# Attention with a window and sinks, then an MLP mixer, on one core: q and k of two more head pairs turned by TensorE, with new orders of work

## The chip, the core and the metric

The kernel runs on one core of a Trainium2 chip. Its engines are TensorE (PE in the profile; PEld is its weight load), VectorE (DVE), ScalarE (ACT), GpSimd (POOL) and SyncE (SP), beside sixteen DMA engines that all queues share. The metric is the device time of one execution in microseconds, the median of several runs. A profiled execution has its own time and, inside it, a span from its first to its last instruction.

## The reference, cut to what matters

```python
# q, k, v: (4, 8, 768, 64) float32, n_sink = 4, window = 128
scores = scale * np.matmul(q, k.transpose(0, 1, 3, 2))
is_sink = pos[None, :] < int(n_sink)
rel = pos[:, None] - pos[None, :]
in_window = (rel >= 0) & (rel < int(window))
scores = np.where(is_sink | in_window, scores, -1000000000.0)
a = softmax(scores);  attn = np.matmul(a, v)         # softmax written out in the reference
x = attn.transpose(0, 2, 1, 3).reshape(4, 768, 512)
h = np.maximum(x.transpose(0, 2, 1) @ w_tok1, 0.0) @ w_tok2   # (512, 768)->(512, 256)->(512, 768)
u = x + h.transpose(0, 2, 1)
out = u + np.maximum(u @ w_ch1, 0.0) @ w_ch2         # 512 -> 1536 -> 512
```

## The kernel before, in words

Work on the attention goes by **pairs** of heads: pair p is batch p // 4 and two of its eight heads, so there are 16 pairs and each batch has four. For a pair, q and k (two heads of 768 rows and 64 columns) are needed turned, with the 2 x 64 columns on the partitions: tiles qT and kT of 128 x 768. Only a band of the scores is computed, three groups g per pair (`scores`), with a further burst for the four sink keys of two pairs at once (`score_sinks`). ACT takes the exponential, DVE masks, and the values follow (`sink_values`, `values`, or `pv` for the first four pairs); DVE divides by the sums and writes x.

After a batch's four pairs come the mixer's steps: `mix_h` and `mix_u` over tokens (u is x plus the result), u is turned to uT, then `v1` (12 x 2 units of four 128x384 products, ReLU on ACT or DVE) and the output product `whole` (24 units of three 128x512 products, added to u by DVE and stored by SP).

**How tiles are turned.** Pairs 0 to 3 arrive by SP as float32 and are cast. From pair 4 on POOL issues loads that cast to bf16 on the way (`load_cast`, L131, two DMAs of 96 KB for q and two for k). Pairs 4 to 7 are turned by TensorE: `transposed` writes 24 small transposes to PSUM (L549), and each of the four quarters of a pair is copied out by ACT (L153) or DVE (L155), the sink columns too (kTs). Pairs 8 to 15 are turned by one DMA each for q and k, which SP issues (L476); the sink columns are then copied out of kT by POOL or DVE (kTs<-kT), so that copy waits in its engine's queue for the DMA to land. The constant `BY_DMA` is the first pair that is turned so; it also sets how the rows of a pair lie over the partitions (`rows_of`: six neighbouring rows in one partition below it, rows 128 apart from it on). u of batches 2 and 3 is turned by DMAs too (L866), that of batches 0 and 1 by TensorE.

**What sets the order.** TensorE's units run in the order of the string `ORDERED`: a letter names a stream and a number the unit in it.

- t, m, s, o: turns, masks, scores and values of pairs 0 to 3; g, h: tokens of batch 0
- a: scores of pairs 4 to 15, three for each, so a12 to a14 are pair 8 and a18 to a20 pair 10
- b: seven for each two pairs: sink scores, then for both pairs sink values and two of values; b0 to b6 are pairs 4 and 5, b14 to b20 pairs 8 and 9
- e: turns by TensorE from pair 4 on: e0 and e1 are q and k of pair 4, e2 pair 5, e3 pair 6, e4 pair 7
- f: u of batch 1 turned; k: tokens of batches 1 to 3, eight each
- c: v1, 24 for each batch; x: output products, 24 for each batch

The loads on POOL go in the order of the string `LOADED`: t is a weight of the tokens, c and d are quarters of w_ch1 and w_ch2, q, k and v with a number are a pair's tiles. q and k have six buffers each (`NQ`), so the load of pair p waits until pair p - 6 has been turned; v has six as well and waits for the values of pair p - 6. POOL has at most eight of its DMAs under way: it waits for the landing of the eighth before. kT has three buffers.

Everything that is not TensorE's (evictions, masks, loads, DMA turns, stores) is put on its queue by a planner, `Plan`: it walks the TensorE order with a cost for each piece and always issues next what can begin first. Its only use is to fix the order in which each engine's instructions are written; each engine then runs its own in that order. A DMA turn costs `TURN` = 1300 ns there, times `CROWDED` while loads are queued.

Of the kernel before, what the change touches and what calls it, by code (L numbers as in the profile page):

```python
# [16 lines left out]
def kernel(  # L17
# [23 lines left out]
    NHP = H // 2  # L41
# [3 lines left out]


    ORDERED = (
# [10 lines left out]
    )  # L58
    ORDER = (1, 2, 7, 6, 4, 5, 3)
    NQ = 6  # L60
    LOADED = (
        "v1 t0 v3 v2 t1 q4 k4 c3 q5 c0 k5 c2 v4 d1 k7 k6 v5 c1 q6 q7 d0 v6 q8 d2 k9 k8 v7 d3 q9 k11 v8 q13 k10 v9 "
        "k15 v12 q10 k14 q11 k12 q12 v10 v11 v13 q14 v14 k13 q15 v15"
    )
    BY_SEVEN = ()
    BY_DMA = 2 * NHP
    MASKED_BY_PE = [(p, g) for p in range(NHP) for g in range(NT // 2) if (p, g) != (NHP - 1, 0)]

    singles = ctx.enter_context(tc.tile_pool(name="singles", bufs=1))
# [17 lines left out]
    def bank(tag, *shape, dtype=FP32, slot=None):  # L87

        n = given[tag].pop(0) if slot is None else slot
        if tag == "sc":  # L90
            return sc[n]
        size = 1
        for x in shape:
            size *= x
        flat = sc[n // 2][:, n % 2].rearrange("p b c d -> p (b c d)")
        flat = (flat if dtype == FP32 else flat.bitcast(dtype))[:, 0:size]
        names = "abc"[:len(shape)]
        return flat.rearrange(
            f"p ({' '.join(names)}) -> p {' '.join(names)}", **{x: v for x, v in zip(names, shape)},
        )  # L100

    in_order = tc.keep_in_program_order
    pairs = [(b, hp) for b in range(B) for hp in range(NHP)]


    def rows_of(pidx, n):

        b, hp = pairs[pidx]
        rows = (q, k)[n][b, 2 * hp:2 * hp + 2]
        if pidx >= BY_DMA:  # L110
            return rows.rearrange("h (j p) d -> p h j d", p=P)
# [33 lines left out]
    def mm(*args, **kwargs):  # L145
        in_order(nc.tensor.matmul(*args, skip_group_check=True, **kwargs))  # L146
# [4 lines left out]
    def copy(e, out, in_):  # L151
        if e == "ACT":
            in_order(nc.scalar.activation(out, in_, AF.Copy))  # L153
        else:
            in_order({"DVE": nc.vector, "POOL": nc.gpsimd}[e].tensor_copy(out=out, in_=in_))  # L155
# [98 lines left out]
    FIRST = 1800.0  # L254
    LANES = 8
    TURN, STORE = 1300.0, 700.0
    CROWDED = 2.4

# [21 lines left out]
    class Plan:  # L280
# [90 lines left out]
        def run(self, units):  # L371
            units = list(units)
            while units or self.pending:
                o = self.other()
                t = self.start_pe(units[0][1]) if units else None
                if o is not None and (t is None or o[0] <= t):
                    op = self.pending.pop(o[1])
                    op.fn(o[2])
                    self.free[o[2]] = o[0] + op.cost[o[2]]
                    op.done = self.free[o[2]] + op.lag  # L380
                    if op.traffic:
                        crowded = self.queue > self.free["SP"] + 1000.0
                        self.sent = max(self.sent, self.free["SP"]) + op.traffic * (CROWDED if crowded else 1.0)
                        self.queue = max(self.queue, self.free["SP"]) + op.traffic
                        op.done = self.sent + 600.0
                    if op.loads:
                        self.queue = max(self.queue, self.free[o[2]] + FIRST) + op.lag
                        op.done = self.queue + 500.0
                        self.landings += [op.done] * op.loads
                    continue  # L390
                assert t is not None, "no unit can begin"
                self.commit_pe(units.pop(0)[1], t)
# [55 lines left out]
    def prepare(p):  # L448
# [22 lines left out]
        tiles["kT", p] = kT  # L471
        if p >= BY_DMA:
            def turn(e, n):
                if not n:
                    tiles["qT", p] = att_pool.tile([P, S], BF16, name="qT2")
                in_order(nc.sync.dma_start_transpose(  # L476
                    out=(kT if n else tiles["qT", p]).rearrange("c (t p) -> c t p", t=NT),
                    in_=bfs[p, n].rearrange("p t h d -> p (t h d)"),
                ))
# [305 lines left out]
    def group(b, g):  # L785
        return g * DM // 2, DM // 2
# [50 lines left out]
    def mix_u(b, g, s0, n, by_pe=False):  # L837
        c0, cn = group(b, g)

        def run():  # L840
            ps_u = tiles["ps_u", b, g, s0] = bank("mx", n, cn)
            for st in range(n):
                if by_pe:
                    mm(ps_u[:, st], ident, x_sb[b][:, s0 + st, c0:c0 + cn], start=True, stop=False)
                for tt in range(NTOK):
                    mm(
                        ps_u[:, st], w_tok2[:, tt, ts(s0 + st, P)], tiles["mix", b][0][:, tt, c0:c0 + cn],
                        start=(tt == 0 and not by_pe), stop=(tt == NTOK - 1),
                    )

        def add(e):
            if by_pe:
                return copy(e, u_part(b, g, s0, n), tiles["ps_u", b, g, s0])
            in_order(nc.vector.tensor_tensor(  # L854
                out=u_part(b, g, s0, n), in0=tiles["ps_u", b, g, s0], in1=x_sb[b][:, s0:s0 + n, c0:c0 + cn], op=ALU.add,
            ))

        op = Op({"DVE": 150.0 + 1.05 * n * cn}, add)
        op.urgent = (1 + g) * (b == 0)
        if by_pe:  # L860
            op.cost["ACT"] = 190.0 + 0.78 * n * cn
        done["u", b, g, s0] = op
        then = [op]
        if pairs[BY_DMA][0] <= b:
            def turn(e):
                in_order(nc.sync.dma_start_transpose(  # L866
                    out=tiles["mix", b][2].rearrange("c (g t p) -> c g t p", g=2, p=P)[:, g, 2 * s0:2 * (s0 + n)],
                    in_=u_part(b, g, s0, n).rearrange("p t c -> p (t c)"),
                ))

            then.append(Op({"SP": 1230.0}, turn, [op], traffic=TURN))
            for half in range(s0 // QH, (s0 + n - 1) // QH + 1):
                done.setdefault(("uT", b, half), []).append(then[-1])
        return unit(n * (NTOK + by_pe) * cn * 0.432, run, done["h", b, g] + [done["tok2"]], {"mx": [[op]]}, then)
# [71 lines left out]
    def attention_and_tokens():  # L946

        scored, out, turns, turned, tokens = [], [], [], [], []
        first, end = NHP, len(pairs)
        for p in range(first, end):  # L950
            prepare(p)
            plan.pending.append(sink_rows(p))
        turns += [turn(first, n) for n in range(2)]
        turns += [burst(transposed(p)) for p in range(first + 1, BY_DMA)]
        for p in range(first, end):
            scored += [burst(scores(p, g)) for g in range(NT // 2)]
            if p % 2:
                out.append(burst(score_sinks(p)))
                for n in (p - 1, p):
                    out += [burst(sink_values(n)), *(values(n, i) for i in range(2))]  # L960
        for b in range(1, B):
            for g in range(2):
                tokens.append(mix_h(b, g, 0, NTOK))
                tokens += [mix_u(b, g, st, 2) for st in range(0, NT, 2)]
                if pairs[BY_DMA][0] > b:
                    turned.append(burst(turned_u(b, g)))
        return scored, out, turns, turned, tokens

# [372 lines left out]
```

## Time and profile before

| | |
|---|---|
| median of 3 runs | 207.49 us (206.03 to 208.84) |
| time of the profiled execution | 208.19 us |
| its span | 206.4 us, 4881 instructions |
| PE busy | 197.1 us (95%), 2021 matmuls |
| DVE, ACT, POOL busy | 106.1, 101.9, 72.0 us |
| mean granted TensorE clock | 0.987 |
| DMA | 26.28 MB in 92550 packets |
| loads issued by POOL, issue to landing | 7.7 to 9.1 us (medians of the q, k, v and w_ch groups) |
| DMA turns of q and k, issue to landing | 7.5 and 8.2 us (medians) |
| DMA turns of u, issue to landing | 2.4 us (median) |

How to read it: PE is nearly always busy, so the end is set by what PE has to do and by the few places where it waits. The other engines matter where PE waits for them. The time of an execution is its span and some 1.8 us around it.

### The profile page before, as it was taken

The page shows a single profiled execution, that of the slowest core. Times are in us where ns is not written, and L with a number is a line of the kernel's source. Part 1 is how long each engine was busy: PE and PEld are TensorE (multiplying, and loading weights), DVE is VectorE, ACT ScalarE, POOL GpSimd, SP SyncE. Part 2 cuts the span into 40 slices and gives each one's busy share as a digit, 9 for nine tenths or more (in the row PEclk, how much of TensorE's full clock was granted, in tenths as well). Part 3 has the DMA queues.
Part 4 walks back from the last instruction along what each step waited for, and adds up shares of the span by engine and source line. Part 5 has one row for each costly group of instructions (what it writes and reads, how often), then busy time and mean ns, then how long its engine had stood idle before and what let it go on. Part 6 is the DMA issues. An engine that isn't in the chain of part 4 may idle for free.

```text
span 206.4 us, 4881 instructions
## 1 busy us (share of the span) xinstructions
PE 197.1 (95%) x2021; PEld 115.4 (56%) x2021; DVE 106.1 (51%) x240; ACT 101.9 (49%) x176; POOL 72.0 (35%) x106
## 2 busy tenths in 40 slices
PE   6999998999995999999999999999999999999992
PEld 2345894566562565566656474566665455654451
DVE  4586877657873637266466776537612423001221
ACT  4598667877860351378754433486551003763000
POOL 6479868997815993676000000000000000000000
PEclk9999999999999699999999999999999999999998
DMA  6999999999999999999995764300122421100223
GB/s 209 253 274 179 175 186 181 175 173 175 125 144 127 222 135 181 180 167 174 138 87 114 156 154 95 137 0 3 37 44 68 110 102 51 54 0 0 102 102 105
DMA packets 92550, 26.28 MB, mean 127 GB/s; under 512 B 82544, under 2 KB 89584, under 8 KB 92528
## 3 DMA queue, kind: packets, MB, share of 16 engines
q0 software_dynamic: 67232, 11.80, 74.9%
q1 hardware_dynamic: 25296, 14.17, 30.4%
q8 instruction: 16, 0.26, 0.5%
q14 instruction: 6, 0.05, 0.1%
HBM read 26.75 MB, written 6.29 MB: 160 GB/s over the span
## 4 chain that ended last, share of the span: by engine, by line
PE 78%; DMA 18%; POOL 1%; SPq 0%; issue 0%; DVE 0%
PE ps L146 76%; DMA q_f<-in_q_dram 6%; DMA kT<-k_bf 5%; DMA w_tok<-in_moe_w_tok_dram 4%; DMA k_bf<-in_k_dram 4%; PE ps L549 1%; PE ps L519 0%; SPq L118 0%; POOL k_bf L131 0%; POOL q_bf L155 0%; POOL w_ch L164 0%; PE ps L149 0%; DVE o_sb L1175 0%
## 5 line engine op out<-in xcount | busy, mean ns | idle before, releaser
L146 PE MATMUL ps<-w_ch,v1T 128*128 128x512 bf16 (+2 forms) x312 | 69.4, 369 | 0.0
L146 PE MATMUL ps<-uT,w_ch 128*128 128x384 bf16 x384 | 68.6, 326 | 0.0
L159 ACT ACTIVATE v1T<-ps 128x384 bf16<-128x384 f32 x78 | 37.8, 491 | 41.2 <-PE ps L146 38.0
L620 ACT ACTIVATE pT<-ps 128x1024 bf16<-128x1024 f32 (+1 forms) x48 | 44.1, 956 | 22.3 <-PE ps L146 22.2
L146 PEld LDWEIGHTS <-w_ch 128*128 128x128 bf16 x384 | 35.8, 98 | 23.4 <-issue 0.7
L146 PEld LDWEIGHTS <-v1T 128*128 128x128 bf16 x312 | 29.2, 99 | 28.4 <-issue 1.9
L1140 DVE TENSOR_TENSOR o_sb<-ps,u_sb 128x512 f32<-128x512 f32 x23 | 15.8, 688 | 38.1 <-PE ps L146 24.0
L131 POOL DMA_DIRECT2D q_bf<-in_q_dram x24 | 19.9, 836 | 5.8 <-DMA v_aug<-in_v_dram 3.2
L146 PEld LDWEIGHTS <-w_tok 128*128 128x128 bf16 x192 | 18.2, 98 | 5.6 <-issue 0.9
L131 POOL DMA_DIRECT2D k_bf<-in_k_dram x24 | 19.9, 840 | 2.2 <-PE ps L149 1.0
L638 DVE TENSOR_TENSOR pT<-pT,mask_main 128x1024 bf16<-128x1024 bf16 (+1 forms) x24 | 14.8, 620 | 11.1 <-ACT pT L620 11.0
L146 PE MATMUL ps<-qT,kT 64*64 64x192 bf16 (+3 forms) x288 | 16.2, 254 | 2.2 <-DMA kT<-k_bf 2.2
L139 POOL DMA_DIRECT2D v_aug<-in_v_dram x16 | 16.6, 1042 | 3.5 <-PE ps L146 1.7
L146 PEld LDWEIGHTS <-pT 128*128 128x128 bf16 x352 | 14.7, 98 | 3.4 <-DMA v_aug<-in_v_dram 0.2
L854 DVE TENSOR_TENSOR u_sb<-ps,x_sb 128x512 bf16<-128x512 f32 x20 | 13.4, 682 | 6.2 <-PE ps L146 4.9
L146 PE MATMUL ps<-v_aug,pT 128*128 128x65 bf16 x352 | 15.8, 193 | 0.0
L146 PE MATMUL ps<-h1T,w_tok 128*128 128x256 bf16 x96 | 14.3, 273 | 0.0
L161 DVE TENSOR_SCALAR v1T<-ps 128x384 bf16<-128x384 f32 x18 | 9.7, 554 | 8.3 <-PE ps L146 8.2
L638 DVE TENSOR_TENSOR pT<-pT,mask_first 128x1024 bf16<-128x1024 bf16 x13 | 8.9, 684 | 8.6 <-ACT pT L620 8.6
L747 DVE TENSOR_TENSOR x_sb<-ps,recip 128x384 bf16<-128x384 f32 x24 | 13.0, 550 | 0.5
L155 POOL COPY kTs<-kT 64x4 bf16<-64x4 bf16 x12 | 2.2, 182 | 30.7 <-DMA kT<-k_bf 30.4
L146 PEld LDWEIGHTS <-kT 64*64 64x64 bf16 (+1 forms) x288 | 6.6, 102 | 11.1 <-issue 6.5
(68 smaller groups left out, 135.3 us busy)
## 6 DMA issues: line engine op xcount, KB each, us to landing
out_dram<-o_sb SPq DMA_DIRECT2D x23, 256.0 KB, 2.8
v_aug<-in_v_dram POOLq DMA_DIRECT2D x16, 192.0 KB, 9.1
w_ch<-in_moe_w_ch_dram POOLq DMA_DIRECT2D x8, 384.0 KB, 8.2
q_bf<-in_q_dram POOLq DMA_DIRECT2D x24, 96.0 KB, 8.5
k_bf<-in_k_dram POOLq DMA_DIRECT2D x24, 96.0 KB, 7.7
q_f<-in_q_dram SPq DMA_DIRECT2D x4, 384.0 KB, 6.0
k_f<-in_k_dram SPq DMA_DIRECT2D x4, 384.0 KB, 6.4
w_tok<-in_moe_w_tok_dram POOLq DMA_DIRECT2D x2, 384.0 KB, 8.3
```

What stands on the lines that cost most here:

```text
L131: in_order(nc.gpsimd.dma_start(out=out[:, h], in_=rows[:, h]))
L139: in_order(nc.gpsimd.dma_start(out=v_aug.rearrange("p i t d -> p (i t) d")[:, :, 0:D], in_=v[b].rearrange("h s d -> (h s) d")[2 * hp * S:2 ...
L146: in_order(nc.tensor.matmul(*args, skip_group_check=True, **kwargs))
L155: in_order({"DVE": nc.vector, "POOL": nc.gpsimd}[e].tensor_copy(out=out, in_=in_))
L159: in_order(nc.scalar.activation(out, in_, AF.Relu))
L161: in_order(nc.vector.tensor_scalar_max(out=out, in0=in_, scalar1=0.0))
L549: in_order(nc.tensor.transpose(ps[x][:, n, j], bfs[p, n][rows, j], ident[rows, rows]))
L620: in_order(nc.scalar.activation(part(tiles["pT", p][:, :, ds(2 * g, 2)]), of_keys(tiles["ps_s", p, g])[:, :, 0:width(g)], AF.Exp, scale=scale,
L638: in_order(nc.vector.tensor_tensor(out=pt, in0=pt, in1=m, op=ALU.min))
L747: in_order(nc.vector.tensor_tensor(out=x_sb[b][:, :, ds((2 * hp + i) * D, D)], in0=tiles["ps_o", p, i][:, :, 0:D], in1=tiles["recip", p, i ...
L854: in_order(nc.vector.tensor_tensor(out=u_part(b, g, s0, n), in0=tiles["ps_u", b, g, s0], in1=x_sb[b][:, s0:s0 + n, c0:c0 + cn], op=ALU.add,))
L1140: in_order(nc.vector.tensor_tensor(out=o_sb.rearrange("p (g c) -> p g c", g=2), in1=u_rows(b, st), in0=tiles["ps_out", b, st].rearrange("p ...
```

## The change

Four things change. `BY_DMA` goes from 8 to 10, so that q and k of pairs 8 and 9 are turned by TensorE, in two new units e5 and e6, their rows lie as those of pairs 4 to 7 do, and ACT and DVE copy them out of PSUM; their four DMA turns are gone. A second constant, `U_BY_DMA` = 2, keeps u of batches 2 and 3 with the DMAs as before. In the planner a DMA turn among loads costs 2.8 times one alone instead of 2.4, and it holds up the loads behind it by 1.1 times its cost instead of once. Both order strings are new. The planner's constants and the strings move instructions; they change no instruction's own work.

```diff
     ORDERED = (
-        "t0-1 m0-1 s0 m2 s1 t2-3 s2 m3 s3 m4 o0 s4 m5 t4 s5 o1 t5 o2 m6 t6 s6 o3 m7 t7 s7 m8 o4 s8-10 m9-10 "
-        "s11-12 g0 o5-6 g1 o7-8 g2 e0-1 g3 h0-1 g4-5 h2-3 g6 h4-5 g7 h6 e2 a0 h7 c0-2 b0 a1 c3-5 b1 a2-3 c6-8 b2 "
-        "c9 a4-5 c10-12 b3 c13-14 e3 b4 c15-16 b5 c17 b6 c18-19 e4 a6-7 k0 c20 x0 b7 a8 c21-22 k1 x1 a9 b8 c23 b9 "
-        "k2 x2 b10 a10-11 x3-8 a12-13 b11-13 x9-11 k3 x12 k4 x13 a14 f0 a15 b14 x14 k5-6 x15-17 k7 x18-20 f1 a16 "
-        "b15 x21-22 c24-27 x23 c28 b16 c29-30 b17 c31-34 a17 b18 a18 c35-37 b19-20 c38-39 a19-20 b21 c40-43 k8 "
...
+        "t0-1 m0-1 s0 m2 t2 s1-2 t3 m3 s3 m4 o0 m5 s4 t4 s5 o1 t5 m6 o2 s6 t6 m7-8 t7 s7-8 o3-4 m9 s9-10 m10 "
+        "s11-12 g0 o5-6 g1 o7-8 g2 e0-1 g3 h0-1 g4-5 h2-3 g6 h4-5 g7 h6 a0 e2 a1 c0-2 h7 c3-5 b0 a2-4 c6-13 a5 b1 "
+        "e3 c14-15 b2 c16-17 b3 c18 a6-7 b4-5 x0 c19-21 e4 a8 c22 b6 c23 x1 b7 e5 a9 x2 k0 x3 a10 b8 a11 b9 x4-8 "
+        "b10 a12 b11 e6 b12 x9-10 k1 x11 k2-3 b13 x12-14 a13 f0 a14 k4 x15 a15 x16 k5-7 x17 a16 b14 x18-20 f1 b15 "
+        "a17 x21-22 b16 x23 c24-26 b17 c27-28 b18 a18-19 c29-31 b19-21 a20 c32-39 k8 c40 a21 b22 a22 b23 c41 b24 "
...
     LOADED = (
-        "v1 t0 v3 v2 t1 q4 k4 c3 q5 c0 k5 c2 v4 d1 k7 k6 v5 c1 q6 q7 d0 v6 q8 d2 k9 k8 v7 d3 q9 k11 v8 q13 k10 v9 "
-        "k15 v12 q10 k14 q11 k12 q12 v10 v11 v13 q14 v14 k13 q15 v15"
+        "t0 v1 v3 v2 t1 k4 q4 c2 k5 q5 c0 v4 q6 q7 c3 c1 k6 q8 d0 v5 k8 k7 q10 d3 d1 d2 v6 v7 q9 k9 k13 k10 k12 "
+        "v8 k11 q13 v13 k14 q11 v9 q15 v12 q12 v14 v10 v11 v15 q14 k15"
     )
     BY_SEVEN = ()
-    BY_DMA = 2 * NHP
+    BY_DMA = 10
+    U_BY_DMA = 2
...
-    CROWDED = 2.4
+    CROWDED, HELD_UP = 2.8, 1.1
...
-                        self.queue = max(self.queue, self.free["SP"]) + op.traffic
+                        self.queue = max(self.queue, self.free["SP"]) + op.traffic * (HELD_UP if crowded else 1.0)
...
-        if pairs[BY_DMA][0] <= b:
+        if b >= U_BY_DMA:
...
-                if pairs[BY_DMA][0] > b:
+                if b < U_BY_DMA:
```

10 rows, old and new, of the table ORDERED are left out of this document.

## The prediction

> **What bounds the kernel now.** I read the page's busy times first, then the chain that ended last, then TensorE's waits, and last the timeline around the longest of them.
>
> ```profile
> PE 197.1 (95%) x2021; PEld 115.4 (56%) x2021; DVE 106.1 (51%) x240; ACT 101.9 (49%) x176; POOL 72.0 (35%) x106
> PEclk9999999999999699999999999999999999999998
> ```
>
> PE is busy for 95% of the span and the granted clock dips in one slice, the fourteenth. So only PE's waits, that dip, and PE's own work are there to be won. The chain from 30 us on, in order of time:
>
> ```profile
> 31.81 0.35 PE ps L549 x12
> ...
> 50.36 5.30 PE ps L146 x50
> 55.66 10.55 DMA kT<-k_bf
> 66.21 0.05 issue
> 66.26 8.59 PE ps L146 x79
> ...
> 82.40 120.01 PE ps L146 x1006
> ```
>
> From 32 us to the end the chain is TensorE but for one piece: a DMA turn of a kT, issued at 55.66 and landed at 66.21. TensorE's waits say the same: one of 2.2 us on it, one of 0.7 us on a load of k, the rest in the first 11 us.
>
> ```profile
> PE ps L146 <- DMA kT<-k_bf: 2.2, 1, 2.2
> ...
> PE ps L549 <- DMA k_bf<-in_k_dram: 0.7, 1, 0.7
> ```
>
> The timeline of PE around the long one (start, us, instruction):
>
> ```profile
> 59.97 4.06 PE L146 MATMUL ps<-w_ch,v1T 128*128 128x512 bf16 x18
> 66.26 0.68 PE L146 MATMUL ps<-qT,kT 64*128 64x256 bf16 x12 [2.23 <-DMA kT<-k_bf]
> 66.87 0.30 PE L146 MATMUL ps<-v_sink,pT_sink 64*128 64x65 bf16 x8
> 67.10 0.84 PE L146 MATMUL ps<-v_aug,pT 128*128 128x65 bf16 x22
> 67.78 3.79 PE L146 MATMUL ps<-w_ch,v1T 128*128 128x512 bf16 x9
> 71.38 0.63 PE L146 MATMUL ps<-h1T,w_tok 128*128 128x256 bf16 x4
> ```
>
> These are x3 to x8, then a12 and a13, the first scores of pair 8, the first pair turned by DMAs. The row at 67.78 shows the rest of the price: nine 128x512 products take 3.60 us until the next row starts at 71.38, where eighteen took about 3.9 before. The windows give the granted clock there:
>
> ```profile
> 66.00:68.00 2.00, 1.74 (x44) 1.22 (x45) 1.34 (x5) 1.31 (x2) 2.00 (x3) 1.00 2.21 174
> 68.00:71.40 3.40, 3.40 (x10) 1.20 (x9) 2.17 (x5) 1.01 (x3) 3.40 (x5) 0.50 1.83 222
> ```
>
> The last three numbers are clock, DMA share and GB/s: half clock for 3.4 us just after the wait. After 82 us no wait of PE is left, so whatever is gained or lost before reaches the end undiminished.
>
> **What is removed.** (1) The wait ahead of a12. A unit of three 128x512 products takes 0.65 us on PE here (x to x in the timeline), so six from 59.97 end at 63.87; a12 began at 66.26: 2.39 us. (2) The half clock after it: 3.60 us for three units that take 1.95: 1.65 us. Pairs 8 and 9 no longer have a DMA turn, so neither can come from there. (3) The 0.7 us row. In the order before, e2 (pair 5) came right behind h6 and the load of k5 was late: e2 and its wait took 1.18 us from 30.79 where the next such unit took 0.36: 0.82 us. In LOADED a quarter of w_ch1 that lay ahead of k5 now lies behind it (its landing came 1.9 us after the landing before it), and a0 stands between: k5 and q5 land at about 29.6 against a start of about 31.1. Sum removed: 4.86 us.
>
> **What is added.** Two units e5 and e6, each 24 transposes; the row of pairs 6 and 7 (L549 x24) starts the next unit 0.36 us later: 0.72 us. Two more changes between small and large products in the order, 0.10 us each by the units that follow one (0.74 against 0.65): 0.20 us. The output of e5 and e6 costs ACT and DVE eight copies of 128x384 (0.49 on ACT, 0.55 on DVE) and four sink copies of 0.16: about 4.8 us in all. I put it at nothing: between 51 and 66 us DVE is busy 9.76 and ACT 7.47 of 15 us, and DVE stood still for 3.36 of them because its own copy of the sink columns waited behind a DMA turn; that wait goes with the turn. If the cover were gone, PE would wait for its banks by at most the last copy, some 0.5 us for each unit. Four POOL copies (0.18 each) go from a queue in which one of them held up the loads for 4.88 us.
>
> DVE's row in the timeline that bears this out:
>
> ```profile
> 66.23 0.36 DVE L155 COPY kTs<-kT 64x4 bf16<-64x4 bf16 x2 [3.36 <-DMA kT<-k_bf]
> ```
>
> Sum without new waits: 0.92 - 4.86 = **-3.94 us**, and adding PE's measured durations unit by unit along the new order gives the same within 0.3 us.
>
> **What the new orders put at risk.** Summing the durations along the new order from a start of a0 at 30.8 gives the times at which PE reaches each unit; the trace's landing times give what a load takes of the queue: between successive landings 1.27 us for a whole q or k, 1.53 for a v, 1.87 for a quarter of w_ch. Up to k4 and q4 the same loads precede as before (landed at 25.0).
>
> - x1 needs d1. Behind 25.0 come c2, c0, c3, c1, d0, d3, d1 (7 x 1.87), nine q or k (11.4) and two v (3.1): 52.6. PE reaches x1 at 53.3. x2 needs d2, 54.5, and is reached at 55.1. Slack 0.7 and 0.6 us.
> - b8 (sink values of pair 6) needs v6, about 56.0, and two copies of 0.25; reached at 58.0.
> - e6 needs q9 and k9: 54.5 + two v + two q or k = 60.1, and later by what the one DMA turn of that stretch, q of pair 10, holds them up. Between the landings at 54.00 and 67.28 the old queue carried 7.1 us of loads in 13.3: 6.2 us for three turns, 2.1 each. So 62.2, against 62.8.
> - o3 needs v1, which now lies behind t0 and lands at about 18.3 where o3 is reached at about 17.9; a wait of up to 0.4, partly taken up because ACT's exponentials set the pace there.
>
> Four places with less than 1 us to spare, on landings that I know to about 1 us. I cost them from both sides: 0 if all land as computed, 2.5 us if each is a microsecond late and none of the waits reaches the 2.2 us that the trace shows to be enough for half clock. I take **0.9**, since the waits are in one queue and a wait at x1 pays for those behind it. The new orders also bring DMA turns of pairs 10 to 15 nearer to or further from their use; by the table a18 is reached at 84.7 and k10 lands at about 64, its turn at 64 + 2 + 8.5, so ten microseconds are left. Bounds: 0 and the price of rival C.
>
> Sum: -3.94 + 0.9 = **-3.0 us**. The profiled execution took 208.19 us, of which 206.4 are its span; the median of the runs is 207.49, 0.7 less. Against the median the forecast is **204.4 us**, span 203.4.
>
> [...] The row first: after 2.23 us without a matmul the clock was 0.50 for 3.4 us, which cost 1.65. [...]
>
> **The rivals.**
>
> A: no new waits at all. Then -3.94: 203.5 us against the median. For it: the landings as computed are all earlier than their use. Against: the slack is below 1 us four times.
>
> B: the wait moves to e6. For it: q9 and k9 now lie behind six other loads in a row, and kT of pair 10 or stores may hold them up by another 2.1 or 4.2. Then e6 waits 1.5 to 3.6 us, with the half clock in the longer case: -3.0 + 1.5 to -3.0 + 3.6 + 1.65, that is 205.9 to 209.7, around 206.7. Against: only q10 can be turned before then.
>
> C, the other side: sink columns of a pair from 10 on are copied on DVE, behind a DMA turn that lands late. The planner reckons with 1.3 x 2.8 us and some margin for a turn among loads, the trace shows 7.5 to 8.5 from issue to landing. DVE then stands as at 62.87 to 66.23, no bank is freed by it, and PE follows: 2.39 + 1.65 = 4.0 us each. Once gives 208.5, a little slower than before; twice gives 212.5. It decides from the second one on. For it: six pairs are still turned so, and PE comes to them 4 us sooner. Against: in the profile before two of eight such copies were on DVE, and only the first waited.
>
> D: the change does not do what it says, that is, pair 8 is late for its loads rather than its turn. q8 and k8 land at about 46.5 by the same table and e5 is reached at 54.4, so this is unlikely; it would give 207 to 208.5.
>
> E: the slow stretch at 68 us comes by itself and stays, so that only the wait goes: -3.0 + 1.65 = -1.4, 206.1 us. [...] Against: it is the only dip between the start and the last slice, and it begins 1.7 us after the only long wait.
>
> **How the numbers follow.** Chances: the forecast (within 0.8 us) 0.40, A 0.21, B 0.17, C 0.15 (one third of it twice), D 0.04, E 0.03. Two per cent of the median, about what a measurement of this kernel can tell from no change, is 4.15 us: faster than that needs under 203.34, which is half of A, the lower edge of the forecast, and gains in the first 30 us that I cannot see: 0.24. Slower needs over 211.64: C twice, and what I have not thought of: 0.12. Within: 0.64. The range leaves out the top of C and the bottom of A: 202.8 to 208.6; the forecast's own is 203.6 to 205.2.
>
> **What would show it.** Right: in the changed profile no wait of PE on kT<-k_bf between 50 and 80 us and no slice of PEclk below 9 but the last; L549 with 60 instead of 36 products of each of q and k; 12 instead of 16 turns at L476; a12 reached at 62 to 63.5 instead of 66.26; last matmuls about 3 us sooner. Waits of PE on w_ch, v_aug or k_bf, each under 1.5 us, would be the 0.9. Wrong: a new wait of 2 us or more followed by half clock (B at e6, C on DVE's kTs<-kT), or the old distance from a12 to the end grown by more than the two units.

## The result, and the profile after

The changed kernel takes 204.72 us (median of 20 runs, 203.85 to 209.12), the kernel before 207.45 us (median of 20, 205.25 to 208.84 but for one execution of 683.66). The ratio is 0.990, 95% interval 0.9875 to 0.9929. The ratio leaves out the longest executions of each kernel, of which the kernel before has more; the medians alone give 0.987.

The profile on record of the changed kernel is of its longest execution, 209.12 us. A usual one, 204.38 us, was profiled in the run after_again below, and these lines of its page answer to those of before:

```profile
span 202.7 us, 4976 instructions
...
PE 194.6 (96%) x2069; PEld 115.2 (57%) x2069; DVE 108.7 (54%) x250; ACT 106.6 (53%) x183; POOL 71.4 (35%) x100
...
PEclk9999999999999999999999999999999999999999
```

There are 48 matmuls more than before and no slice of slow clock. The chain in order of time (start, us, what) has no DMA from 30 us on:

```profile
44.20 7.90 PE ps L147 x88
52.10 0.46 PE ps L550 x24
52.56 2.97 PE ps L147 x32
55.53 0.46 PE ps L550 x24
55.98 8.16 PE ps L147 x93
64.15 0.35 PE ps L550 x24
...
79.58 120.16 PE ps L147 x999
```

The last three L550 rows are e4, e5 and e6. The timeline of PE around the place where pair 8 had waited:

```profile
59.97 3.40 PE L147 MATMUL ps<-w_ch,v1T 128*128 128x512 bf16 x15
63.20 0.50 PE L147 MATMUL ps<-v_aug,pT 128*128 128x65 bf16 x11
63.63 0.39 PE L147 MATMUL ps<-qT,kT 64*128 64x256 bf16 x4
```

The row at 63.63 is a12, 2.63 us earlier than the 66.26 of before, and no wait stands ahead of it. The long execution differs in one place. There DVE's copy of the sink columns of pair 10 waited behind a DMA turn, and PE behind DVE (two engines of the profile on record):

```profile
72.61 0.56 DVE L156 COPY uT<-ps 128x768 bf16<-128x768 bf16 x1
75.23 0.80 DVE L156 COPY kTs<-kT 64x4 bf16<-64x4 bf16 x2 [2.06 <-DMA kT<-k_bf]
76.06 0.69 DVE L639 TENSOR_TENSOR pT<-pT,mask_main 128x1024 bf16<-128x1024 bf16 x1
76.67 0.68 DVE L162 TENSOR_SCALAR h1T<-ps 128x512 bf16<-128x512 f32 x1
...
77.41 2.74 PE L147 MATMUL ps<-h1T,w_tok 128*128 128x256 bf16 x12 [2.08 <-DVE h1T L162]
```

Twelve products of 128x256 that take 1.47 elsewhere take 2.74: its windows show half clock again, 0.51 from 77.3 to 80.7. That is rival C of the prediction, once; the same execution also waited 0.73 us for w_ch at x2. By the prediction's own signs this profile shows rival C, and the usual execution shows the forecast (its a12, at 63.63, lies just past the 62 to 63.5 named).

### The profile page after: what moved, and what is told of

Read it like the earlier page. It is cut to its first block, busy times and chain, and to the rows that moved or that the text cites. A ratio compares the mean times of both kernels' runs of the same rounds, so it can differ in the third digit from the quotient of the medians.

```text
span 207.4 us, 4957 instructions
## 1 busy us (share of the span) xinstructions
PE 195.5 (94%) x2050; PEld 116.1 (56%) x2069; DVE 108.5 (52%) x250; ACT 106.4 (51%) x183; POOL 72.2 (35%) x100
## 4 chain that ended last, share of the span: by engine, by line
PE 65%; DMA 27%; POOL 3%; issue 2%; DVE 1%; SPq 0%; ACT 0%
PE ps L147 64%; DMA v_aug<-in_v_dram 9%; DMA q_f<-in_q_dram 6%; DMA w_ch<-in_moe_w_ch_dram 5%; DMA kT<-k_bf 4%; DMA w_tok<-in_moe_w_tok_dram 4%; POOL q_bf L132 2%; POOL w_ch L165 1%; SPq L119 0%; DVE kTs L156 0%; POOL q_bf L156 0%; DVE h1T L162 0%; DVE qT L156 0%; PE ps L520 0%; PE ps L550 0%
## 5 line engine op out<-in xcount | busy, mean ns | idle before, releaser
L147 PE MATMUL ps<-w_ch,v1T 128*128 128x512 bf16 (+2 forms) x295 | 67.2, 363 | 1.7 <-DMA w_ch<-in_moe_w_ch_dram 0.7
L160 ACT ACTIVATE v1T<-ps 128x384 bf16<-128x384 f32 x80 | 39.1, 491 | 39.1 <-PE ps L147 35.0
L147 PEld LDWEIGHTS <-w_ch 128*128 128x128 bf16 x384 | 36.3, 98 | 24.8 <-DMA w_ch<-in_moe_w_ch_dram 0.6
L147 PEld LDWEIGHTS <-v1T 128*128 128x128 bf16 x312 | 28.5, 98 | 27.3 <-issue 1.8
L147 PEld LDWEIGHTS <-w_tok 128*128 128x128 bf16 x192 | 18.8, 101 | 8.6 <-DVE h1T L162 2.6
L639 DVE TENSOR_TENSOR pT<-pT,mask_main 128x768 bf16<-128x768 bf16 (+1 forms) x23 | 14.0, 615 | 9.6 <-ACT pT L621 9.6
L147 PE MATMUL ps<-h1T,w_tok 128*128 128x256 bf16 x96 | 15.6, 291 | 2.1 <-DVE h1T L162 2.1
L162 DVE TENSOR_SCALAR v1T<-ps 128x384 bf16<-128x384 f32 x16 | 8.7, 555 | 6.5 <-PE ps L147 5.8
L147 PE MATMUL ps<-x_sb,w_tok 128*128 128x256 bf16 x96 | 12.0, 273 | 0.0
```

Source lines behind the costliest of these rows:

```text
L160: in_order(nc.scalar.activation(out, in_, AF.Relu))
L162: in_order(nc.vector.tensor_scalar_max(out=out, in0=in_, scalar1=0.0))
L639: in_order(nc.vector.tensor_tensor(out=pt, in0=pt, in1=m, op=ALU.min))
```

## The experiments

Lines of code are those of the changed kernel (one more than before in the helpers).

**Turning alone, turns_alone.** Old orders and constants:

```diff
-        "... x2 b10 a10-11 x3-8 a12-13 b11-13 x9-11 k3 x12 k4 x13 a14 f0 ..."
+        "... x2 b10 a10-11 e5 x3-8 a12-13 b11-13 x9-11 k3 x12 k4 x13 e6 a14 f0 ..."
-    BY_DMA = 2 * NHP
+    BY_DMA = 10
+    U_BY_DMA = 2
```

> The old order strings and the old planner constants; only the first pair turned by DMAs goes from 8 to 10, with e5 put ahead of x3 and e6 ahead of a14. Theory T (the wait of pair 8 on its DMA turn and the half clock behind it are what went; the orders are not needed for that): -2.4 - 1.65 + 0.9 = -3.1 us, ratio to the kernel before 0.985; no wait of PE on kT between 50 and 80 us. Rival O (the new orders of loads and units are what brought the time): the loads are as late as before, e5 or e6 waits for them, ratio 0.995 or more.

Measured: 206.52 us against 207.18, ratio 0.9997 (0.9958 to 1.0036); the medians give 0.997. The wait on kT and the half clock are gone, but PE stood 1.59 us at a15 for ACT's copy of kT of pair 9:

```profile
74.67 0.40 PE L147 MATMUL ps<-qT,kT 64*128 64x256 bf16 x4 [1.59 <-ACT kT L154]
```

The loads behave as theory T says: with no DMA turn among them, v8 landed at 62.2 instead of 67.3. Neither theory is borne out by the time alone; e6 stood too close to its use, as the next run bears out.

**The same with e6 earlier, turns_alone2.**

```diff
-        "... x9-11 k3 x12 k4 x13 e6 a14 f0 ..."
+        "... x9-11 e6 k3 x12 k4 x13 a14 f0 ..."
```

> As turns_alone (old orders, pairs 8 and 9 turned by TensorE), but e6 stands ahead of k3 instead of ahead of a14, some 3 us earlier on PE. In turns_alone PE stood 1.6 us at a15 because ACT had not yet copied kT of pair 9 out of PSUM. Theory T (turning alone is worth what the change brought, if the copies have time): the wait at a15 is gone, -1.6 us against turns_alone's 206.5, so 204.9, ratio 0.988 to 0.990, as the changed kernel. Rival O (the orders bring part of it): 206.0 or more, ratio 0.995.

Measured: median 208.48 against 207.08, with two levels: two executions at 205.25 and 205.5, ten at 207.67 to 209.19. The medians give 1.007; the ratio made as above, 0.9999 (0.9945 to 1.0052), rests on four of the twelve. The wait at a15 is gone, but theory T missed the time by 3.6 us. The profile, of a short execution, showed DVE idle for 2.61 us at kTs<-kT and PE then waiting 1.08 us for u. That pointed to rival C of the prediction.

**A longer execution of it, turns_again.**

> turns_alone2 once more, for a profile of a long execution. Theory C: DVE stands 3 us or more at kTs<-kT near 69 us, PE waits 2 us or more at f0 or a15, and half clock follows for 3.4 us. Rival: no such row, but more waits of PE on loads.

Measured: one execution of 206.86 us, between the levels. DVE and PE in its timeline:

```profile
68.20 0.68 DVE L1141 TENSOR_TENSOR o_sb<-ps,u_sb 128x512 f32<-128x512 f32 x1
72.76 0.34 DVE L156 COPY kTs<-kT 64x4 bf16<-64x4 bf16 x2 [3.87 <-DMA kT<-k_bf]
73.13 0.56 DVE L156 COPY qT<-ps 128x384 bf16<-128x384 bf16 x1
73.72 0.69 DVE L855 TENSOR_TENSOR u_sb<-ps,x_sb 128x512 bf16<-128x512 f32 x1
...
74.46 0.32 PE L520 MATMUL ps<-ident,u_sb 64*64 64x64 bf16 x16 [2.34 <-DVE u_sb L855]
```

A copy of 4 columns holds DVE for 3.87 us; the copy of qT of pair 9 and u stand behind it, and f0 on PE waits for u. No half clock followed in this one, contrary to the expectation. The half clock would add 1.65 and give the 208.5 of the upper level; that sum is an inference, no profile of that level was taken. The mean clocks on record bear it out in part: one stretch of 3.4 us at half clock takes 0.008 off the mean of such a span, and eight of the ten long executions of turns_alone2 have 0.992 or less; but two, 207.67 and 208.53, have 1.000 and are long without it.

**That copy off DVE, turns_alone2_pool.**

```diff
-                {"POOL": 300.0, "DVE": 300.0}, sinks_of, done["kT", p] + [("sk", p - NHP)],
+                {"POOL": 300.0}, sinks_of, done["kT", p] + [("sk", p - NHP)],
```

> As turns_alone2, but the sink columns of pairs 10 to 15 are copied by POOL alone. Nine of twelve executions of turns_alone2 took 207.7 to 209.2, two 205.3 and 205.5; in the profile of a short one DVE stood 2.61 us at the sink columns of pair 10, behind the DMA turn of its kT, and PE then waited 1.1 us for u. Theory C (that copy is what keeps the old orders from gaining): all executions at 204.5 to 205.5, ratio 0.988. Rival (the old order of units and loads is itself slower by 3 us in most executions): two levels again, median near 208, ratio 1.000.

Measured: 204.38 us, six executions from 203.68 to 204.72; against 206.59 the ratio is 0.9896 (0.9855 to 0.9936). One level, and the changed kernel's time, with the old orders and the old constants. Each measured against the kernel before beside it, the medians went from 1.007 to 0.989 by this one edit, which also lets the planner shift a few rows on ACT and DVE. So turning pairs 8 and 9 on PE, with these copies on POOL, is enough for the gain without the new orders, and the copy on DVE was what hid it. POOL stood at the copies too, once for 6.75 us while loads were still to be issued, but from 33 us on PE waited for nothing. The kernel before with only the copies moved was not run; in its profile PE waits for the landing of kT itself, which that move would not bring forward, so that it would gain little is argued, not shown.

**The orders alone, orders_alone.**

```diff
-    BY_DMA = 10
+    BY_DMA = 8
-        "... b7 e5 a9 x2 ... b11 e6 b12 ..."
+        "... b7 a9 x2 ... b11 b12 ..."
```

> The new orders and constants, but pairs 8 and 9 are still turned by DMAs (e5 and e6 left out of the order). k8 lands some 7 us earlier by the new order of loads, so its turn is issued at about 47 and may land at 55 to 57, ahead of a12 at 62. Theory T: the wait at a12 is gone here too, but four more DMA turns hold up the loads behind them by 2.1 us each: x1 and x2 wait 2 to 4 us for w_ch2; ratio 0.995 to 1.005. Rival O: no such wait, and PE saves the 0.7 us of the two units: ratio 0.985 or less.

Measured: 212.73 us, ratio 1.0263 (1.0214 to 1.0313). Both theories expected less. The turn of kT of pair 8 was issued at 46.5, right behind its load, and landed at 58.0, and DVE was queued behind it:

```profile
52.29 0.56 DVE L156 COPY qT<-ps 128x384 bf16<-128x384 bf16 x1 [1.06 <-ACT v1T L160]
58.03 0.34 DVE L156 COPY kTs<-kT 64x4 bf16<-64x4 bf16 x2 [5.18 <-DMA kT<-k_bf]
...
55.62 0.81 PE L147 MATMUL ps<-w_ch,v1T 128*128 128x512 bf16 x2 [1.43 <-DMA w_ch<-in_moe_w_ch_dram]
...
59.01 0.39 PE L147 MATMUL ps<-qT,kTs 64*32 64x512 bf16 x2 [2.26 <-DVE qT L156]
...
65.68 0.56 PE L147 MATMUL ps<-v_sink,pT_sink 64*128 64x65 bf16 x8 [1.26 <-ACT v_sink L154]
```

So x1 waits for w_ch, as T had it (1.4 us rather than 2 to 4); a second wait of 2.26 is on DVE, with half clock behind it (twelve products of 128x256 from 61.30 took 2.18 where 1.47 is usual), and a third of 1.26 on ACT's copy of v_sink. With 1.65 for the half clock these are 6.6 us. The span is 7.5 us longer than in after_again, though 0.8 us of turns are left out, so some 1.7 us are not accounted for. The new orders by themselves are no gain: rival O is out.

**The constants, constants_alone.** The changed kernel with `CROWDED, HELD_UP = 2.4, 1.0`.

> The changed kernel with the planner's old constants (2.4 instead of 2.8, 1.0 instead of 1.1), so that only the places of DMA turns, loads and copies on their queues move. If the constants only describe what the orders already avoid: 204.7 within 0.5 us, ratio 0.990. If they keep DVE's and POOL's queues out of the way of late turns: more waits behind kT on DVE, half clock, 206.5 to 209.

Measured: 204.74 us, ratio 0.9883 (0.9848 to 0.9917): the changed kernel's. The new constants move rows on four queues and no time that could be measured.

**The changed kernel with the copies on POOL, sinks_on_pool.** The edit of turns_alone2_pool made to the changed kernel; PE's and ACT's orders stay.

> The changed kernel with the sink columns of pairs 10 to 15 copied by POOL alone: PE's and ACT's orders are the same, two copies go from DVE's queue to POOL's. If the wait on DVE's copy is an accident of some executions (rival C of the prediction): the median is that of the changed kernel within 0.3% (ratio to before 0.990), and no execution shows a half clock near 77 us. If DVE's copy costs in every execution: 0.985. If POOL, blocked behind the turn, brings the loads late: v9 is missed at b18, ratio 0.995 or more.

Measured: 204.58 us, six executions from 204.06 to 204.68, ratio 0.9862 (0.9818 to 0.9905). The median stays, as the first expectation had it, and POOL did not make v9 late. None of the six comes near the 205.66 to 209.12 of five of the changed kernel's twenty, but six are few: with five in twenty long, six in a row without one come by chance 18 times in 100. One of the six (204.63) has a mean clock of 0.990, and no profile tells where it lost it. That rival C costs some executions of the changed kernel is seen in the profile on record; that this edit takes it away there is not shown.

**Idle work in the wait, warm_wait.** The kernel before, with ten products of ones between x8 and a12:

```diff
+    def fill():
+        ps = bank("mx", 4 * P)
+        for _ in range(10):
+            mm(ps, ones[:, 0:P], ones, start=True, stop=True)
+    streams["w"] = [unit(0, fill, [], {"mx": [[]]})]
-        "... x3-8 a12-13 ..."
+        "... x3-8 w0 a12-13 ..."
```

> The kernel before with ten 128x512 products of ones put between x8 and a12, 2.16 us of idle work inside the wait of 2.4 us; every other engine's order is as before. If the half clock at 68 us comes from the wait: it is gone, -1.65 us, ratio 0.992, and the wait on kT shrinks to some 0.2 us. If it comes by itself (rival E): clock 0.5 stays in one slice and the ratio is 1.000.

Measured: 206.04 us against 207.18, ratio 0.9942 (0.9911 to 0.9973). The timeline and the windows of PE:

```profile
63.86 2.32 PE L146 MATMUL ps<-ones 128*128 128x512 bf16 x9
66.11 0.68 PE L146 MATMUL ps<-qT,kT 64*128 64x256 bf16 x12
...
67.64 2.10 PE L146 MATMUL ps<-w_ch,v1T 128*128 128x512 bf16 x8
```

```profile
68.00:71.40 3.40, 3.35 (x22) 2.04 (x21) 3.23 (x7) 0.87 (x3) 3.40 (x5) 1.00 1.85 242
```

a12 begins where it did (66.11 against 66.26), and the clock is 1.00 where it was 0.50. All twelve executions have a mean clock of 0.997 or more; of the 23 of the kernel before measured beside them nine have 0.992 or less. Work that nobody needs makes the kernel faster, so the half clock came from the wait; rival E is out. The gain of 1.1 us is less than 1.65, since most executions of the kernel before had no half clock to lose.

**The kernel before again, before_again.**

> The kernel before once more, to see how the wait of pair 8 varies: the profile on record has 2.2 us and half clock in an execution of 208.19, the median is 0.7 less. If the wait is what varies: a wait on kT between 1 and 2.5 us, time 205 to 208.5, and half clock only with the longer wait.

Measured: 206.44 us. Here PE lost time early, 1.92 us at o3 for v1 and half clock from 17.8 on (0.51 up to 21.2), and a0 began 1.75 us later than in the first profile. Yet:

```profile
61.72 4.06 PE L146 MATMUL ps<-w_ch,v1T 128*128 128x512 bf16 x18
66.47 0.68 PE L146 MATMUL ps<-qT,kT 64*128 64x256 bf16 x12 [0.69 <-DMA kT<-k_bf]
```

a12 begins at 66.47 again. In both profiles of the kernel before the landing of that turn, not PE, sets the time of a12 (66.26 and 66.47), and what PE lost ahead of it only made the wait shorter. The wait of 0.69 lies under the 1 to 2.5 us expected, and the half clock came behind another wait, the one at o3.

**The changed kernel again, after_again.**

> The changed kernel once more, since the execution in its profile took 209.12 and 15 of 20 took 203.85 to 205.1. If that wait on DVE's copy is not in a usual execution: no half clock between 60 and 90 us, PE waits of 1 to 1.4 us at o3 and 0.7 us at x2, span 202.5 to 203.3.

Measured: 204.38 us, span 202.7; its lines are shown with the result. No half clock, as expected; the wait at o3 is shorter than expected and the one at x2 is missing:

```profile
PE ps L147 <- DMA v_aug<-in_v_dram: 0.8, 1, 0.8
```

**Two loads moved, v1_first and v1_first_q10_late.** Both from sinks_on_pool:

```diff
-        "t0 v1 v3 v2 t1 k4 q4 c2 k5 q5 c0 v4 q6 q7 c3 c1 k6 q8 d0 v5 k8 k7 q10 d3 d1 d2 v6 v7 q9 k9 k13 k10 k12 "
+        "v1 t0 v3 v2 t1 k4 ..."                                   # both
+        "... v5 k8 k7 d1 d3 d2 v6 v7 q9 k9 q10 k13 k10 k12 "      # the second
```

> The changed kernel with the sink columns on POOL alone and with v1 loaded ahead of the token weight t0, as in the kernel before. In sinks_on_pool PE waited 1.4 us for v1 at o3. If that wait reaches the end: -1.2 to -1.4 us, 203.3, ratio 0.980. If ACT's exponentials set the pace up to 23 us anyhow, as the prediction had it: -0.3 us or less, 204.3.

Measured: 204.50 us, ratio 0.9876 (0.9838 to 0.9915). The wait at o3 went and the time stayed, as the second expectation had it.

> As v1_first, and q10 is loaded behind k9 instead of ahead of d3, with d1 ahead of d3. q10's DMA turn was issued as soon as q10 had landed, at 50 us, among the loads of w_ch2, whose landings then came 2.0 to 2.7 us apart instead of 1.9. If that turn is what made x2 wait (0.8 us in the changed kernel's profile): d1, d2 and v6 land 2 to 3 us earlier, no wait at x1 and x2, and 0 to 0.8 us less than v1_first. If the turn only moves its delay to k13 and k10: the same time as v1_first.

Measured: 203.77 us, six executions from 203.24 to 204.15, ratio 0.9832 (0.9798 to 0.9866), the shortest of all and under the changed kernel. d1 landed at 49.4 instead of 53.7, as expected. But in the profiles the 1.2 us by which its a12 is earlier (62.65 against 63.88) are there at a0 already (30.61 against 31.84), well ahead of q10. So the gain is measured and its cause is open; one profile of each does not tell whether it lies in q10.

## Why the prediction was right, point by point

**The bound and the wait.** Right. The prediction named one wait of PE and the half clock behind it, and both went with pair 8's DMA turn. From 80 us on the chain is PE in both kernels, and the start of the last product unit moved from 201.56 to 198.89: -2.67 us, forecast -3.0.

**The terms.** The first c unit begins at 32.54 us in the profile of before and at 32.56 in after_again (one small unit ahead of it differs, h7 before and a1 after). From there to the start of the last product unit before takes 169.02 us, of which 2.23 are the wait and 1.65 the half clock; after_again takes 166.33, with no wait. So these two terms went as forecast, and 1.2 us came, where the prediction wrote 0.92. Of them 0.8 are the two units (0.36 for e5 and 0.45 for e6, where 0.72 stood), so the term that was too small is mainly "two more changes between small and large products": 0.20 stood there, and 0.4 came. The third term did not reach the end: the wait at e2 is gone, but as much was lost ahead of the first c unit. -2.23 - 1.65 + 1.2 = -2.7.

**Where the new waits were.** Wrong in place. In the usual execution they were in the first 26 us; x1, x2, b8 and e6 waited for nothing. At o3 a wait of up to 0.4 was forecast; it was 0.6 to 1.6 in the five profiles with these loads, and v1_first, without it, took the same time. So the 0.9 of new waits and the 0.82 to be won at e2, neither of which reached the end, cancelled each other in the forecast. One step failed though it cost little: q10's turn was counted against q9 and k9 alone. It was issued at 49.5, as soon as q10 had landed, and held up d1 (53.2 instead of 52.6), d2 (55.6 instead of 54.5) and v6 (58.1 instead of 56.0). In the execution on record x2 did wait 0.73 us for w_ch. The price of a turn was right: the old loads from k8 to v8 took 13.3 us with three turns among them and 7.3 in turns_alone2 with none, 2.0 each (forecast 2.1).

**The scale.** The sum was taken from the median, though it had been read from an execution 0.7 us longer than the median, and with a half clock that most executions do not have. Of the 56 executions of the kernel before measured beside the experiments, 16 have a mean clock of 0.992 or less; their medians are 208.2 to 208.8 us, those of the others 206.5 to 206.9. So the median execution had no such stretch to lose. Against the others the changed kernel and its variants with the same orders (204.4 to 204.7) gain some 2.1 us, where the forecast without its 1.65 would have been 1.4; no profile of such an execution of the kernel before was taken, so what makes the difference is open. Nor is the wait the same each time: it is what is left between PE and a landing near 66.3 (2.23 and 0.69). That the forecast of 204.4 came so close to 204.72 is thus in part luck. Span against span the two profiles differ by 3.7 us, of which 1.1 lie behind the last product (4.85 against 3.79 us to the end; 4.04 in before_again).

**The copies at nothing.** "I put it at nothing" held in the new order and failed in the old one: with e6 just ahead of its use PE lost 1.59 us (turns_alone).

**Rival C.** It had 0.15. It is real, and for the old orders it decides, as turns_alone2 and turns_alone2_pool show together: ten long executions of twelve with the copy on DVE, none of six without. In the changed kernel it shows in full in the execution on record, the only one of twenty with a mean clock below 0.998: 2.08 of wait and some 1.65 of half clock, 3.7 us against a forecast of 4.0. The four from 205.66 to 206.81 have full clock, and their cause is open.

**The wait and the half clock.** The row that the prediction went by, 2.23 us and then half clock, was borne out as an example and not as a measure. Waits of PE of 1.92 (before_again), 2.08 (the profile on record), 2.23 (before) and 2.26 us (orders_alone) were followed by half clock, 3.4 us of it in the first three; one of 2.34 (turns_again, mean clock 1.000) was not. In the clock record of two profiles the stretch of full clock ahead of the half clock lasted a whole multiple of 3.413 us, the length of the half clock itself: in before 58.03, from 9.98 to 68.01, which is 17 times; in the profile on record 71.68, from 5.66 to 77.34, 21 times. What decides whether a wait is followed by half clock was not shown.

## What to carry to other kernels

The wait at the end of a DMA chain took up here what happened ahead of it (a0 began 1.75 us later in before_again, a12 at 66.47 instead of 66.26): first find which landing sets it, then count its whole price, the clock included, and only then what lies in front. Before a small copy is put on a busy in-order engine, ask what it waits for: four columns behind a DMA turn cost up to 3.7 us here, the 48 products that replaced four turns 0.8, and moving that copy to GpSimd brought with the old orders what the newly found orders brought. Test the parts of a change apart: here turning alone gave nothing until e6 stood earlier and that copy was off DVE, and the orders alone lost 2.6%, the longest of their waits behind the same copy. And look whether the execution in the profile is a usual one: here neither of the two first profiled was.

## What the runs showed of the hardware that was not expected

A DMA turn of 192 KB among loads took 5.3 to 8.2 us from issue to landing (the medians of q and k in before and after_again) and 11.5 once in orders_alone; two turns of q issued when no load was left, at 108.25 and 117.87 us in the profile on record, took 2.80 and 2.75. A turn took 2.0 us of the loads' queue (13.3 us from k8 to v8 with three turns, 7.3 with none), where the load of a whole q or k, which also writes 192 KB, takes 1.27 between landings. So it is the time taken from the queue in which a turn costs more than a load; from issue to landing the loads of after_again took about as long (6.9 to 8.3).

Whether a wait of some 2 us brings half clock is not settled by its length alone (2.34 did not, 1.92 did), so a wait of about that length cost 2.3 us in one execution (turns_again) and 3.9 in another (2.23 and 1.65, before).
